# A cached attention decode step: loads of both caches moved from two queues to one, in 8 MB pieces, with a ring for the keys

## The chip, the cores and the metric

One core of a Trainium2 chip runs the whole program. The metric is the device time of one execution in microseconds. Times here are medians of several runs, and a profile shows one further execution.

## The reference

`B` = 2 sequences, one new token each, `D` = 512; 32 query heads of `DH` = 128 share 8 key/value heads (4 to 1); the caches hold `SK` = 32,768 positions. All is float32.

```python
xn = layernorm(x)
q  = (xn @ wq) split into 32 heads            # wq: 512 x 4096
scores = q . k_cache * DH**-0.5               # k_cache: 2 x 8 x 32768 x 128
o  = softmax(scores) . v_cache                # v_cache: the same shape
s  = o (heads side by side) @ wo              # wo: 4096 x 512
h  = relu(xn @ w1 + b1)**2                    # w1: 512 x 1792
g  = silu(h @ w2 + b2)                        # w2: 1792 x 512
out = x + s * g                               # 2 x 512
```

Each cache is 268 MB, and every byte of both is read once. The weights add 24 MB.

## The kernel before

A **stretch** `s` (0 to 15) is one pair of key/value head and sequence, `hkv, b = divmod(s, B)`. Its 32,768 positions are cut into `NCH` = 4 chunks of 8,192: 4 MB of keys and 4 MB of values, 64 positions (32 KB) on each of 128 partitions.

**Loads.** Two pools hold two 4 MB buffers each: `kpool` for keys (and at the end for `wo`), `vpool` for values (and at the start for `wq`, `w1`, `w2`). A Python list `loads` fixes one order; `issue()` walks down it as long as the next load's pool has a free buffer, and `give(pool)` is called where a buffer's last reader has been written down. Keys and weights are issued from SP's DMA queue (`nc.sync`, `load_k` at L90, `load_w1` L101, `load_w2` L106, `load_wo` L113 to L118); values from ACT's (`nc.scalar`, `load_v` at L96). On the profile SP's queue is q1 and ACT's q10. Each queue issues in order; an issue waits in its queue until the readers of the buffer are done. The small inputs `b1`, `b2` and `x` are issued from SP ahead of `wq` (L72 to L74).

**Scores (L244, L249).** The products need keys with `DH` on the partitions, in blocks of 32. `nc.vector.transpose` turns 32 x 32 blocks; one instruction (L244) turns 1,024 elements per partition, 8 positions x 128. Eight of them do a chunk, into eight small tiles `kt`. TensorE multiplies each with the query, spread over a mask `qz` that POOL fills (L228), in products of 256 columns (L249); four products run side by side, one per group of 32 output partitions. A float32 product is two records in the profile.

**Softmax (L256 to L272).** When the fourth chunk's scores stand in PSUM: maximum on DVE (`rm`, L256), a transpose on TensorE (`mx_ps`, L258), small DVE steps (`mh`, `mm`, `nm`), then the exponential on ACT (`p`, L268). `probs` (L281 to L290) transposes `p` on TensorE into `pT_ps` and copies it to `pT` on ACT (two copies of 512 per stretch), and computes the scale `rs` per head.

**Values (L305 to L317).** For each 4 MB chunk 16 products of 512 columns add into `o_ps`; behind a stretch's last one `o_sb` is copied out, scaled and transposed into `oT`.

**Order.** A loop over `n` (chunks) writes down scores of chunk `n`, `probs` of the stretch before (at its first chunk), values of chunk `n - 4`, and `softmax` at the fourth chunk. The Tile framework builds each engine's list from this, and may set ready work ahead of work that waits; on the chip every engine goes through its list in order. `mlp_up` and `mlp_down` (the gate) come in at `n` = 1 and 2.

**End.** `project` (L379) multiplies `oT` by `wo`, heads 0 to 27 first; the last four heads go in three pieces of columns (`PIECES`), each followed by the product with `gate` (L389), a fold of the four partition groups on TensorE (L390) and a copy (L391); then one DMA writes the output (L392).

Of the kernel before, what the change touches and what calls it, by code (L numbers as in the profile page):

```python
# [9 lines left out]
F32 = mybir.dt.float32  # L10
# [4 lines left out]
P = 128  # L15

NG = 4
RUN = 64
CHUNK = P * RUN
NC = 2
NO = 8
KBUFS = 2
VBUFS = 2
PIECES = ((0, 256), (256, 384), (384, 512))
# [3 lines left out]
def gqa_decode_kernel(ctx: ExitStack, tc: tile.TileContext, x, kc, vc, wq, wo, w1, b1, w2, b2, out):  # L33
# [8 lines left out]
    NCH = SK // CHUNK  # L42
    FG = F // NG
    FJ = FG // 32
    WJ = 16
    SCALE = 1.0 / math.sqrt(DH)
    assert NC * 4 * REP == 32 and D == 512 and DH == P and REP * DH == 512 and NCH == 4 and F == P * FJ
# [5 lines left out]
    kpool = ctx.enter_context(tc.tile_pool(name="kpool", bufs=KBUFS))  # L53
    vpool = ctx.enter_context(tc.tile_pool(name="vpool", bufs=VBUFS))
    ktpool = ctx.enter_context(tc.tile_pool(name="ktpool", bufs=8))
# [11 lines left out]

    xt = const.tile([P, D], F32, name="xt")
# [4 lines left out]
    nc.sync.dma_start(b1t, b1.rearrange("(g f) -> g f", g=NG))  # L73
    nc.sync.dma_start(b2t, b2[None, :])  # L74

    tiles = {}
# [5 lines left out]
    def load_wq(i):  # L82
        t = vpool.tile([P, 2, wq.shape[1]], F32, tag="v", name=f"wq{i}")
        nc.sync.dma_start(t, wq.rearrange("(p d) f -> p d f", p=P)[:, 2 * i:2 * i + 2, :])
        return t

    def load_k(m):
        s, u = divmod(m, NCH)
        t = kpool.tile([P, RUN, DH], F32, tag="k", name=f"k{m}")
        nc.sync.dma_start(t, rows(kc, s).rearrange("(p t r) d -> p t r d", p=P, t=NCH)[:, u])  # L90
        return t

    def load_v(m):
        s, u = divmod(m, NCH)
        t = vpool.tile([P, RUN, DH], F32, tag="v", name=f"v{m}")
        nc.scalar.dma_start(t, rows(vc, s)[u * CHUNK:(u + 1) * CHUNK].rearrange("(p r) d -> p r d", p=P))  # L96
        return t

    def load_w1(_):
        t = vpool.tile([P, ND, F], F32, tag="v", name="w1")  # L100
        nc.sync.dma_start(t, w1.rearrange("(p d) f -> p d f", p=P))  # L101
        return t

    def load_w2(_):
        t = vpool.tile([P, FJ, D], F32, tag="v", name="w2")
        nc.sync.dma_start(t, w2.rearrange("(p j) e -> p j e", p=P))  # L106
        return t

    def load_wo(i):
        t = kpool.tile([P, WJ, D], F32, tag="k", name=f"wo{i}")  # L110
        src = wo[i * WJ * P:(i + 1) * WJ * P, :].rearrange("(j p) e -> p j e", p=P)
        if i == 0:
            nc.sync.dma_start(t, src)  # L113
        else:
            nc.sync.dma_start(t[:, :8, :], src[:, :8, :])
            nc.sync.dma_start(t[:, 8:12, :], src[:, 8:12, :])
            for c0, c1 in PIECES:
                nc.sync.dma_start(t[:, 12:, c0:c1], src[:, 12:, c0:c1])  # L118
        return t

    NK = NS * NCH
    loads = [("v", load_wq, 0), ("v", load_wq, 1)]
    for m in range(NK + NCH):
        if m < NK:
            loads.append(("k", load_k, m))
        if m == 1:
            loads.append(("v", load_w1, 0))
        if m == 2:
            loads.append(("v", load_w2, 0))
        if m >= NCH:  # L130
            loads.append(("v", load_v, m - NCH))
        if m == NK:
            loads.append(("k", load_wo, 0))
    loads.append(("k", load_wo, 1))
    free = {"k": KBUFS, "v": VBUFS}
    done = [0]

# [278 lines left out]
```

## Time and profile before

| | |
|---|---|
| time, three runs | 1342.0, 1342.37, 1343.8 us; median 1342.37 |
| span of the profiled execution | 1341.7 us |
| HBM read | 561.0 MB |
| packets on q1 (SP) and q10 (ACT) | 15,026 and 9,216 |
| key loads, value loads | 64 and 64, 4,096 KB each |
| DVE transposes (L244) | 512, 587.3 us busy in all |
| score products (L249) | 4,096 records, 372.5 us busy |
| value products (L305) | 2,048 records, 313.2 us busy |

The page of the profile lists each engine's busy time, then the span in 40 equal slices: a digit is the busy share of a slice in tenths, and below it stand the share of the 16 DMA engines and the GB/s that they moved. The chain that ended last is followed back from the last instruction to whatever released each step. A view by windows gives, for each stretch of time, busy time and instruction count per engine, the clock granted to TensorE, the DMA share and GB/s. A row of the timeline has start, duration, engine, line, operation, output<-input and count, and in brackets the idle time before it with what ended it. "x32" at a product means 32 records, which is 16 products.

### The profile page before, as it was taken

What the parts mean: (1) busy time and instruction counts of PE and PEld (TensorE: products, weight loads), DVE (VectorE), ACT (ScalarE), POOL (GpSimd) and SP (SyncE); (2) the same over time, 40 slices, a digit from 0 to 9 for tenths busy, and PEclk for the clock granted to TensorE, in tenths of its full rate; (3) what the DMA queues carried; (4) which work ended last, traced back from release to release, by engine and by line L of the source; (5) the groups of instructions that cost most, each with busy time, mean ns of one, the idle gap of its engine ahead of it and who ended that gap; (6) DMA issues with size and microseconds to landing.
All of it is one profiled execution on the core that took longest, in us unless ns stands there. A gap on an engine that the chain in (4) does not pass through costs nothing.

```text
span 1341.7 us, 15037 instructions
## 1 busy us (share of the span) xinstructions
PE 754.6 (56%) x6702; PEld 277.8 (21%) x6702; DVE 640.7 (48%) x673; ACT 70.4 (5%) x117; POOL 28.0 (2%) x141
## 2 busy tenths in 40 slices
PE   4666366566563456454736656373664637367564
PEld 1212122122221122211212221121221212122121
DVE  3746546455565464454554445455444545544000
ACT  0001000010000000001000000100000010000010
POOL 1000000000000000000000000000000000000000
PEclk9978678767787778786878868686886868788778
DMA  9999999999999999999999999999999999999994
GB/s 393 433 434 381 429 430 423 432 416 424 434 414 432 435 388 431 433 429 434 429 429 434 429 432 429 431 430 433 427 433 431 428 434 426 434 428 426 377 397 211
DMA packets 24305, 561.96 MB, mean 419 GB/s; under 512 B 2217, under 2 KB 3757, under 8 KB 7346
## 3 DMA queue, kind: packets, MB, share of 16 engines
q1 hardware_dynamic: 15026, 292.57, 51.2%
q10 hardware_dynamic: 9216, 268.44, 46.7%
q8 instruction: 52, 0.85, 0.3%
q14 instruction: 11, 0.09, 0.0%
HBM read 561.00 MB, written 0.00 MB: 418 GB/s over the span
## 4 chain that ended last, share of the span: by engine, by line
DMA 62%; PE 18%; DVE 16%; ACT 2%; issue 1%; DVEq 0%; SPq 0%; ACTq 0%
DMA k<-in_A_k_cache 36%; DMA v<-in_A_v_cache 22%; DVE kt L244 15%; PE o_ps L305 12%; PE sc L249 3%; DMA wo<-in_A_wo 3%; PE pT_ps L281 2%; ACT p L268 2%; DMA wq<-in_A_wq 2%; PE l_ps L286 0%; PE q_ps L205 0%; PE qT_ps L216 0%; PE oT_ps L316 0%; PE a_ps L379 0%; DVE mh L260 0%
## 5 line engine op out<-in xcount | busy, mean ns | idle before, releaser
L244 DVE STREAM_TRANSPOSE kt<-k 128x1024 f32<-128x1024 f32 x512 | 587.3, 1210 | 452.4 <-DMA k<-in_A_k_cache 282.9
L249 PE MATMUL sc<-kt,qz 128*32 128x256 f32 x4096 | 372.5, 399 | 144.8 <-DVE kt L244 141.5
L305 PE MATMUL o_ps<-v,pT 128*16 128x512 f32 x2048 | 313.2, 754 | 201.1 <-DMA v<-in_A_v_cache 201.1
L249 PEld LDWEIGHTS sc<-kt,qz 128*32 128x32 f32 x4096 | 155.1, 113 | 360.7 <-DVE kt L244 218.5
L305 PEld LDWEIGHTS o_ps<-v,pT 128*16 128x16 f32 x2048 | 65.1, 114 | 413.2 <-DMA v<-in_A_v_cache 225.8
L281 PE MATMUL pT_ps<-ident,p 128*128 128x128 f32 x128 | 28.6, 395 | 196.4 <-ACT p L268 196.4
L281 PEld LDWEIGHTS pT_ps<-ident,p 128*128 128x128 f32 x128 | 22.7, 206 | 201.3 <-ACT p L268 200.9
L312 ACT COPY o_sb<-o_ps 128x512 f32<-128x512 f32 x16 | 9.4, 587 | 802.7 <-PE o_ps L305 802.7
L228 POOL COPY qz<-qT 32x16 f32<-32x16 f32 x128 | 25.2, 200 | 1047.6 <-PE sc L249 1017.1
L268 ACT ACTIVATE p<-sc,nm 128x1024 f32<-128x1024 f32 x16 | 33.2, 2077 | 189.9 <-DVE nm L265 189.9
L256 DVE TENSOR_REDUCE rm<-sc 128x1 f32<-128x1024 f32 x16 | 19.6, 1225 | 47.6 <-PE sc L249 47.6
L288 DVE RECIPROCAL r<-l_ps 128x4 f32<-128x4 f32 x16 | 2.9, 183 | 54.0 <-PE l_ps L286 54.0
L260 DVE TENSOR_REDUCE mh<-mx_ps 128x4 f32<-128x128 f32 x16 | 4.2, 265 | 40.1 <-PE mx_ps L258 40.1
L282 ACT COPY pT<-pT_ps 128x512 f32<-128x512 f32 x32 | 18.5, 587 | 21.7 <-PE pT_ps L281 21.7
L316 PE MATMUL oT_ps<-rs,o_sb 128*128 128x4 f32 x128 | 18.5, 268 | 1.9 <-ACT o_sb L312 1.9
L316 PEld LDWEIGHTS oT_ps<-rs,o_sb 128*128 128x128 f32 x128 | 17.1, 208 | 10.3 <-issue 6.6
L389 DVE TENSOR_TENSOR a_sb<-gate,a_ps 128x128 f32<-128x128 f32 (+1 forms) x3 | 1.0, 325 | 35.9 <-PE a_ps L379 35.9
L379 PE MATMUL a_ps<-wo,oT 128*32 128x512 f32 (+2 forms) x80 | 10.6, 521 | 12.0 <-DMA wo<-in_A_wo 12.0
L205 PE MATMUL q_ps<-wq,xnT 128*32 128x512 f32 x64 | 10.6, 821 | 9.1 <-DMA wq<-in_A_wq 9.1
L272 DVE TENSOR_SCALAR lh<-selh,l 128x4 f32<-128x4 f32 x16 | 3.7, 229 | 24.2 <-ACT p L268 24.0
L212 DVE COPY qr<-q_ps 128x512 f32<-128x512 f32 x8 | 5.3, 690 | 19.5 <-PE q_ps L205 19.0
L317 ACT COPY oT<-oT_ps 128x4 f32<-128x4 f32 x16 | 2.7, 166 | 140.2 <-PE oT_ps L316 140.2
(66 smaller groups left out, 94.0 us busy)
## 6 DMA issues: line engine op xcount, KB each, us to landing
k<-in_A_k_cache SPq DMA_DIRECT2D x64, 4096.0 KB, 24.7
v<-in_A_v_cache ACTq DMA_DIRECT2D x64, 4096.0 KB, 27.7
wq<-in_A_wq SPq DMA_DIRECT2D x2, 4096.0 KB, 16.7
w<-in_B_w SPq DMA_DIRECT2D x2, 3584.0 KB, 33.6
wo<-in_A_wo SPq DMA_DIRECT2D x1, 4096.0 KB
wo<-in_A_wo SPq DMA_DIRECT2D x1, 2048.0 KB
wo<-in_A_wo SPq DMA_DIRECT2D x1, 1024.0 KB, 17.2
wo<-in_A_wo SPq DMA_DIRECT2D x1, 512.0 KB, 13.2
```

What stands on the lines that cost most here:

```text
L205: nc.tensor.matmul(q_ps[32 * g:32 * g + 32, f, :], xnT[:, d, 0:32], wqt[:, d2, cc * 512:(cc + 1) * 512], start=(d == 0), stop=(d == ND - 1))
L228: nc.gpsimd.tensor_copy(t[:, c, :, lo:lo + REP], qT[32 * a:32 * a + 32, b, hkv].rearrange("p h e -> p e h"))
L244: nc.vector.transpose(r.rearrange("p e o w -> p o e w"), kt[:, lo:lo + NO, :].rearrange("p o (e w) -> p o e w", e=4))
L249: nc.tensor.matmul(sc[s][32 * g:32 * g + 32, t // 2, c0:c0 + 256], qz[s % 2][:, c, e, :], kts[g][:, e].rearrange("p o w -> p (o w)"), star ...
L256: nc.vector.tensor_reduce(rm, sc[s], axis=AX.XY, op=ALU.max)
L268: nc.scalar.activation(p.rearrange("p o w t -> p o t w"), sc.pop(s).rearrange("p b (t o w) -> p o (b t) w", t=2, w=32), AF.Exp, bias=nm, s ...
L281: nc.tensor.transpose(t_ps[:, j * P:(j + 1) * P], p[:, 4 * i + j].rearrange("p w t -> p (w t)"), ident)
L282: nc.scalar.copy(sb[:, :, 4 * i:4 * i + 4, :].rearrange("p r o h -> p o r h"), t_ps.rearrange("p (o r h) -> p o r h", o=4, h=REP))
L305: nc.tensor.matmul(o[32 * g:32 * g + 16, :], pT[s][:, r0, 4 * i:4 * i + 4, :].rearrange("p o h -> p (o h)"), vt[:, lo:lo + 4, :].rearrange ...
L312: nc.scalar.copy(o_sb, o)
L316: nc.tensor.matmul(t_ps[:, :REP], o_sb[:, i * DH:(i + 1) * DH], r4[:, i, :], start=(i == 0), stop=(i == 3))
L379: nc.tensor.matmul(a_ps[32 * g:32 * g + 32, 0, c0:c1], oT[:, hq, :], wot[hq // WJ][:, hq % WJ, c0:c1], start=(hq < NG), stop=(hq >= HQ - 2 ...
```

## The change

The chunks become twice as large, and the loads go through one queue.

- **Half stretches.** A step `m` (0 to 31) is half a stretch: `RUN` = 128 positions per partition, 8 MB of keys and 8 MB of values, each partition's row 64 KB. A key step has two halves of `SLOT` = 64 positions.
- **Buffers.** `kring` holds three halves (12 MB); half `h` goes to slot `h % 3`. Where the two slots of a step are neighbours in order, one 8 MB load fills both, otherwise two 4 MB loads do. `vbuf` is one buffer of 8 MB for the values. `wq`, `w1`, `w2` are views of `vbuf`, `wo` is a view of the first two slots of `kring`, and small work tiles (`scratch`) come out of the `kt` pool, which has 4 tiles of twice the size instead of 8.
- **Queue.** All large loads are issued from SP, in an order written out by hand; `x`, the biases and `x4` (the token laid out on 4 x 2 partitions) from ACT. There is no list and no `give`: the order of the statements is the order of the queue.
- **Products.** One DVE transpose turns 32 of the 128 columns of 64 positions (2,048 elements per partition); score products have 512 columns, half as many as before. `probs` packs `pT` differently and makes eight ACT copies of 64 partitions x 256 per stretch in place of two.
- **Order.** In a step: scores of the first half, load of the next keys, scores of the second half, then `softmax` or `probs`, values of step `m - 2`, load of values `m - 1`, and `head_out` behind a stretch.
- **End.** Values 30 go to two slots of the ring. Values 31 are loaded in two halves, with `wo` between and behind them: heads 0 to 7, then the second half, then 8 to 15, 16 to 23, 24 to 27, 28 and 29, 30, 31. Heads 24 to 31 are multiplied in four pieces of 128 columns into four groups of partitions, so that the result has 128 columns on 8 partitions; `gate` and `x4` have the same layout. Two DMAs write the output.

```diff
+SLOT = 64
+RUN = 2 * SLOT
+NO = 16
...
+    kring = const.tile([P, 3 * SLOT, DH], F32, name="kring")
+    vbuf = const.tile([P, RUN, DH], F32, name="vbuf")
...
+    def load_k(m, halves=False):
+        a, b = slot(2 * m), slot(2 * m + 1)
+        src = k_rows(m)
+        if b == a + 1 and not halves:
+            nc.sync.dma_start(kring[:, a * SLOT:(b + 1) * SLOT, :], src)
+            return
+        for h in range(2):
+            load_k_half(m, h)
...
+    def load_v(j):
+        nc.sync.dma_start(vbuf, v_rows(j))
...
+    def load_wo(h0, h1):
+        nc.sync.dma_start(wo_t[h0 // 16][:, h0 % 16:h0 % 16 + h1 - h0, :],
+                          wo[h0 * P:h1 * P, :].rearrange("(h p) e -> p h e", p=P))
+
+    nc.sync.dma_start(wq_t, wq.rearrange("(p d) f -> p d f", p=P))
+    load_k(0)
...
-    nc.sync.dma_start(xt[:B, :], x2)
+    nc.scalar.dma_start(xt[:B, :], x2)
...
+    nc.sync.dma_start(w1_t, w1.rearrange("(p d) f -> p d f", p=P))
+    load_k_half(1, 0)
+    nc.sync.dma_start(w2_t, w2.rearrange("(p j) e -> p j e", p=P))
...
+    def scores(m, c):
+        s, u = divmod(m, 2)
+        if u == 0 and c == 0:
             sc[s] = big(f"sc{s}")
...
+        kt = kring[:, slot(2 * m + c) * SLOT:(slot(2 * m + c) + 1) * SLOT, :]
+        for e in range(4):
+            r = ktpool.tile([P, SLOT, 32], F32, tag="kt", name=f"kt{m}_{c}_{e}")
+            nc.vector.transpose(r, kt[:, :, 32 * e:32 * e + 32])
             for g in range(NG):
...
+                nc.tensor.matmul(sc[s][32 * g:32 * g + 32, u, :], qz[s % 2][:, c, e, :],
+                                 r[:, g * NO:(g + 1) * NO, :].rearrange("p o w -> p (o w)"),
+                                 start=(c == 0 and e == 0), stop=(c == 1 and e == 3))
...
+            for a in range(2):
+                for y in range(2):
+                    nc.scalar.copy(sb[64 * a:64 * a + 64, :, 4 * i:4 * i + 4, y, :].rearrange("p z o h -> p o z h"),
+                                   v[64 * y:64 * y + 64, :, :, a, :])
...
+    def values(j, vt, cs=(0, 1)):
...
+    def head_out(s):
...
+    def fold(dst, src, start, stop):
+        for j in range(4):
+            nc.tensor.matmul(dst[32 * j:32 * j + 32, 0:P], selg, src[:, j * P:(j + 1) * P], start=start, stop=stop,
+                             skip_group_check=True)
...
+    for m in range(NH):
+        s, u = divmod(m, 2)
+        if u == 0:
+            set_q(s)
+        if m == 1:
             mlp_up()
...
+        scores(m, 0)
+        if m == 0:
+            load_k_half(1, 1)
+        elif m + 1 < NH:
+            load_k(m + 1)
+            if m == 1:
+                mlp_down()
+                load_v(0)
+        scores(m, 1)
+        if u == 1:
             softmax(s)
...
+        if m >= 2:
+            if u == 0:
+                probs(s - 1)
+            values(m - 2, vbuf)
+            if m < NH - 1:
+                load_v(m - 1)
+            if u == 1:
+                head_out(s - 1)
+
+    A = NH - 2
+    nc.sync.dma_start(kring[:, SLOT:3 * SLOT, :], v_rows(A))
+    nc.sync.dma_start(vbuf[:, 0:SLOT, :], v_rows(A + 1)[:, 0:SLOT])
+    load_wo(0, 8)
+    nc.sync.dma_start(vbuf[:, SLOT:RUN, :], v_rows(A + 1)[:, SLOT:RUN])
+    load_wo(8, 16)
...
+    def heads4(h0, h1):
+        for hq in range(h0, h1):
+            for j in range(4):
+                nc.tensor.matmul(acc[32 * j:32 * j + 32, 0:P], oT[:, hq, :],
+                                 wo_t[hq // 16][:, hq % 16, j * P:(j + 1) * P],
+                                 start=False, stop=(hq == HQ - 1), skip_group_check=True)
+
+    probs(NS - 1)
+    values(A, kring[:, SLOT:3 * SLOT, :])
+    load_wo(16, 24)
+    load_wo(24, 28)
+    load_wo(28, 30)
+    load_wo(30, 31)
+    load_wo(31, 32)
+    values(A + 1, vbuf, (0,))
+    heads(0, 8)
+    values(A + 1, vbuf, (1,))
+    heads(8, 16)
+    head_out(NS - 1)
+    heads(16, 24)
+    asb = scratch("a_sb")[:, 0:D]
+    nc.vector.tensor_copy(asb, project)
+    fold(acc, asb, True, False)
+    heads4(24, HQ)
+    fin = const.tile([P, P], F32, name="fin")
+    nc.vector.tensor_mul(fin, gate, acc[:, 0:P])
+    nc.vector.tensor_add(fin, fin, x4)
+    for b in range(B):
+        eng = nc.sync if b == 0 else nc.scalar
+        eng.dma_start(out2[b, :].rearrange("(j e) -> j e", j=ND), fin[b:b + 97:32, :])
```

More of the change, by code (lines that the diff above doesn't have):

```diff
@@ L138, in issue @@
[L138 to L152 removed]
+    nc.gpsimd.memset(x4, 0.0)
+    nc.scalar.dma_start(xt[:B, :], x2)
+    nc.scalar.dma_start(b1t, b1.rearrange("(g f) -> g f", g=NG))
+    nc.scalar.dma_start(b2t, b2[None, :])
@@ L225, in set_q @@
             t = qz[s % 2][32 * a:32 * a + 32]
-            for c in range(NC):
+            for c in range(2):
                 lo = (c * 4 + a) * REP
```

270 lines of the change are left out of this document (82 added, 188 removed).

## The prediction

> **What bounds the kernel now.** I read the page first: busy engines, the slices, bytes read, the chain.
>
> ```profile
> PE 754.6 (56%) x6702; PEld 277.8 (21%) x6702; DVE 640.7 (48%) x673; ACT 70.4 (5%) x117; POOL 28.0 (2%) x141
> ...
> DMA  9999999999999999999999999999999999999994
> GB/s 393 433 434 381 429 430 423 432 416 424 434 414 432 435 388 431 433 429 434 429 429 434 429 432 429 431 430 433 427 433 431 428 434 426 434 428 426 377 397 211
> ...
> HBM read 561.00 MB, written 0.00 MB: 418 GB/s over the span
> ...
> DMA 62%; PE 18%; DVE 16%; ACT 2%; issue 1%; DVEq 0%; SPq 0%; ACTq 0%
> ```
>
> No compute engine is busy much over half the span; the DMA engines are at 9 in every slice but the last. So the question is what rate the stream has and where it falls short. Second view, the DMA queues in three windows: 5 to 35 us (only SP's queue at work), 500 to 1200 (steady) and 1245 to 1255 (only `wo`).
>
> ```profile
> DMA packets 442, 12.91 MB, mean 430 GB/s; under 512 B 48, under 2 KB 48, under 8 KB 48
> ...
> q1 hardware_dynamic: 442, 12.91, 99.7%
> ```
> ```profile
> DMA packets 10354, 301.32 MB, mean 430 GB/s; under 512 B 1140, under 2 KB 1140, under 8 KB 1140
> ...
> q10 hardware_dynamic: 5171, 150.83, 50.2%
> q1 hardware_dynamic: 5149, 149.98, 49.8%
> ```
> ```profile
> DMA packets 1916, 3.88 MB, mean 388 GB/s; under 512 B 23, under 2 KB 23, under 8 KB 1916
> ```
>
> One queue alone, with loads back to back, runs at 430 GB/s, no less than two together; 4 MB loads queued behind each other cost nothing at their seams. In the steady part the two queues carry 150.83 + 149.98 = 300.81 MB in 700 us, 429.7 GB/s. `wo`, in 2 KB rows, goes at 388.
>
> The bytes by shape: keys and values 536.87 MB, `wq` 8.39, `w1` and `w2` 7.34, together 552.6 MB in long rows; `wo` 8.39. At these rates 552.6/0.4297 = 1286.0 us and 8.39/0.388 = 21.6 us: **1307.6 us of streaming** in a span of 1341.7. The other 34 us lie here (windows, then timeline; the last two columns of a window are the DMA share and GB/s):
>
> ```profile
> 112.00:125.00 13.00, 11.93 (x104) 4.87 (x105) 12.23 (x17) 4.58 (x5) 0.00 (x0) 0.84 0.73 291
> 200.00:300.00 100.00, 62.09 (x524) 23.22 (x527) 54.86 (x61) 7.35 (x11) 1.60 (x8) 0.75 0.99 422
> 300.00:400.00 100.00, 62.39 (x601) 22.70 (x597) 58.01 (x57) 3.98 (x6) 3.21 (x16) 0.81 0.99 425
> 400.00:500.00 100.00, 48.76 (x463) 18.04 (x455) 50.98 (x51) 4.02 (x6) 1.60 (x8) 0.74 0.98 420
> 1260.00:1326.00 66.00, 39.46 (x285) 10.66 (x275) 1.35 (x7) 3.98 (x6) 0.00 (x0) 0.82 0.97 397
> 1325.00:1330.00 5.00, 2.61 (x16) 0.64 (x20) 0.00 (x0) 0.00 (x0) 0.00 (x0) 0.79 0.03 13
> ```
> ```profile
> 0.74 0.37 SPq L73 DMA_DIRECT2D b1t<-in_B_b  x1
> 1.73 0.84 SPq L84 DMA_DIRECT2D wq<-in_A_wq  x2
> 2.13 21.33 DMA wq<-in_A_wq
> 1327.39 5.32 PE L305 MATMUL o_ps<-v,pT 128*16 128x512 f32 x32 [4.43 <-DMA v<-in_A_v_cache]
> 1339.52 0.28 SPq L392 DMA_DIRECT2D out<-fin  x1
> ```
>
> Start 2.1 us (bytes flow 0.4 us after the issue at 1.73). The gap near 115: 13 x (1 - 291/430) = 4.2. 200 to 500: 100 x (8 + 5 + 10)/430 = 5.3. Near the end, values and `wo` waiting for buffers: 66 x 33/430 = 5.1. Then the tail: 0.03 of 5 us after 1325 puts the last byte at about 1325.2, and 16.5 us of compute follow. Sum 33.2 of 34.
>
> **The change part by part.**
>
> *Start.* `wq` becomes SP's first instruction (the small inputs go to ACT's queue): bytes from 0.74 + 0.4 = 1.2 us instead of 2.1. The layernorm then waits for `xt` behind long `wq` packets, but `wq` itself lands only near 22 us.
>
> *Rows of 64 KB.* A 32 KB row costs 700 x 16/(10,354 - 34 - 1,140) = 1.220 us (34 are other queues' packets), a 2 KB row 10 x 16/1,916 = 0.0835: a line through both leaves 8 ns fixed per row. Half as many rows save 0.3%, 4 us. No row of this trace is that long. Ends: -8 (twice the fixed part), and +7, the 0.6% by which the steady windows' two queues differ. I take -4, from the nearest row. The Trainium skill, "DMA: Bandwidth & Descriptors", Where 436 GB/s comes from, caps the ports at 435 GB/s; 552.6 MB at that rate would be 1270 us, an estimate, beyond my bound.
>
> *Steady state.* Per step m the one queue carries 8 MB of keys and 8 MB of values, 16.78/0.4297 = 39.0 us. Let T be the last byte of keys m. Values m-2 stream until T+19.5, keys m+1 until T+39.0. The queue is SP's, in order, so each issue must come before the bytes ahead of it run out. The durations:
>
> ```profile
> 990.49 9.13 DVE L244 STREAM_TRANSPOSE kt<-k 128x1024 f32<-128x1024 f32 x8 [7.58 <-DMA k<-in_A_k_cache]
> 1001.62 1.23 DVE L256 TENSOR_REDUCE rm<-sc 128x1 f32<-128x1024 f32 x1 [2.01 <-PE sc L249]
> 946.86 8.27 PE L305 MATMUL o_ps<-v,pT 128*16 128x512 f32 x64
> 971.20 6.14 PE L305 MATMUL o_ps<-v,pT 128*16 128x512 f32 x32 [4.88 <-DMA v<-in_A_v_cache]
> ```
>
> Landing to use is 2.2 us (1325.2 to 1327.39). Keys m+1 need the first half of keys m transposed: 4 transposes of twice the size. The elements are the same, so 9.13 for 4; were all of a transpose its start, 4.6; were strided reading dearer by half, 13.7. I take 9.13, the nearest row, as 4 or 13.7 leave the issue early too. T + 2.2 + 9.1 + 0.4 = T+11.7, 7.8 us early. Values m-1 need the single 8 MB buffer: the second half's transposes end at T+20.4, its products near T+21.7, when values m-2 have landed too; on softmax steps `rm` adds 1.2. The products of 8 MB take 8.3 us (x64 records) to 12.3 (2 x 6.14, low clock): released by T+31 to T+36, 3 to 8 us before T+39.0. So with one buffer and one queue **nothing runs dry**. What hides the wait is the other cache's 19.5 us load; without it each step would lose the values' 8.3 to 12.3 us.
>
> Halved score products (2,048 of 512 columns in place of 4,096 records of 256), fewer weight loads and `values` reordered touch only PE, which has room: 0. Eight ACT copies of 256 per `probs` replace two of 512:
>
> ```profile
> L282 ACT COPY pT<-pT_ps 128x512 f32<-128x512 f32 x32 | 18.5, 587 | 21.7 <-PE pT_ps L281 21.7
> L317 ACT COPY oT<-oT_ps 128x4 f32<-128x4 f32 x16 | 2.7, 166 | 140.2 <-PE oT_ps L316 140.2
> ```
>
> each between 0.166 and 0.587, about 0.38: 3.0 us, up from 1.2, beside the loads; they touch the end only through the 3 us of room above.
>
> Ring slots, weight views and half loads share tiles with what still runs. Waits go by region, not by tile:
>
> ```profile
> 1299.27 0.59 ACT L282 COPY pT<-pT_ps 128x512 f32<-128x512 f32 x1 [0.27 <-PE pT_ps L281]
> 1299.57 4.10 PE L305 MATMUL o_ps<-v,pT 128*16 128x512 f32 x32
> ```
>
> The product reads the first half of `pT` while the second is still being written. So sharing costs 0.
>
> *Early gaps* (4.2 + 5.3) and the mixing near the end (5.1) go with the order of need. `w1` waits for the query products, done by about 33 us, while `k0` streams until 40.
>
> *Tail.* `wo` is queued between and behind the last values, so small pieces of `wo` land last.
>
> ```profile
> 1332.84 0.59 ACT L312 COPY o_sb<-o_ps 128x512 f32<-128x512 f32 x1 [32.99 <-PE o_ps L305]
> 1333.48 1.05 PE L316 MATMUL oT_ps<-rs,o_sb 128*128 128x4 f32 x8 [0.76 <-ACT o_sb L312]
> ```
> ```profile
> L379 PE MATMUL a_ps<-wo,oT 128*32 128x512 f32 x56 | 8.1, 609 | 12.0 <-DMA wo<-in_A_wo 12.0
> L379 PE MATMUL a_ps<-wo,oT 128*32 128x128 f32 x16 | 1.4, 282 | 0.0
> L389 DVE TENSOR_TENSOR a_sb<-gate,a_ps 128x128 f32<-128x128 f32 (+1 forms) x3 | 1.0, 325 | 35.9 <-PE a_ps L379 35.9
> ```
>
> Behind the last half of the values come 6.3 MB of `wo`, 16.2 us. Beside them PE has that half's products (4.1 to 6.1), `head_out` (0.59 + 1.05 + 0.17), heads 8 to 24 (16 x 8.1/28 = 4.6), copy and fold (about 1.3) and seven narrow heads at up to 4 x 1.4/8 = 0.7 each: 17 to 19, against 16.2. That is level, or some 2.5 late; I take level, since the 0.7 is of products that stood alone between DVE's steps, and keep +2.5. After the last byte: landing 2.2, the last head 0.7, product with `gate` and sum 2 x 0.325, output from issue to end 1341.7 - 1339.5 = 2.2: 5.7 instead of 16.5.
>
> **Sum:** 1.2 + (1286.0 - 4) + 21.6 + 5.7 = 1310.5 us of span; the median before is 0.7 above its profiled span (1342.37 against 1341.7), so **1311 us**.
>
> **The rivals.** *Gaps at the softmax.* Before, the list puts the next keys' transposes ahead of the softmax:
>
> ```profile
> 1019.91 2.05 ACT L268 ACTIVATE p<-sc,nm 128x1024 f32<-128x1024 f32 x1 [17.13 <-DVE nm L265]
> 1022.02 1.97 PE L281 MATMUL pT_ps<-ident,p 128*128 128x128 f32 x8 [19.29 <-ACT p L268]
> ```
>
> PE stands 19 us behind a late `p`. Kept so, `p` comes at T+2.2+18.3+0.7+2.0 = T+23.2, `pT` at T+28.2, values end at T+40.5 at the low clock, the issue at T+40.9: 1.9 us x 15 steps = 28: **up to 1339**. At the full clock values end 4 us sooner and nothing is lost, so half of this case lies below 1330. Against: `softmax` now stands ahead of the values and has 15 us before the next keys.
>
> *Values behind the next keys (slower).* At the 10 steps whose next keys come as two 4 MB loads, PE's list may take the first half's products before values m-2. That half lands at T+29.3+2.2, its transposes end at T+40.6, values at T+48.9: the stream is empty from T+39.0 to T+49.3, 10 us x 10, **1414**. It decides from the point where values end after T+38.6. Against: in one queue the values always land first.
>
> *Long rows at equal pitch.* Were the rate that of the slowest steady window, 420 GB/s, 552.6 MB would take 1315.7 us: **1345**. Against: keys (pitch 128 KB) and values (32 KB) share the engines 49.8 to 50.2. The Trainium skill, same page, Latency and other measured facts, has copies with 512 KiB between rows at 207 GB/s where 214 is full; by that ratio the long rows would cost 43 us more, an estimate. No row here shows such a fall.
>
> *The change doesn't do what it says:* rows cut to 32 KB give 1315, inside the forecast's own range.
>
> **How the numbers follow.** Forecast 0.76 (1304 to 1318); softmax gaps 0.09, nearly all of it faster; values behind keys 0.09, slower; pitch 0.06, half of it within 0.2%, half slower. 0.2% is about what this measurement can tell. Faster 0.84, same 0.04, slower 0.12. The range goes from 1303 (the -8 end and a little less) to 1330; beyond it lie half of the softmax case and the two slower ones, 0.045 + 0.09 + 0.06, just under 0.2.
>
> **What would show it.** Right: GB/s near 430 in all slices from the second on, no early dip; SP's waits long, yet DMA share 1.00; half as many long packets; last `wo` byte some 5 to 6 us before the end. Wrong: windows of a step with a DMA share under 0.95 (values late), or share 1.00 at fewer GB/s (rows), or PE still at heads when the last piece lands.

## The result, and the profile after

The changed kernel takes **1314.17 us** (median of 4 runs, 1313.68 to 1315.37), the kernel before 1343.09 (4 runs, 1342.0 to 1345.11) on the same chip: a ratio of **0.9779, interval 0.9765 to 0.9793**. That is 28.9 us off. The profiled executions say the same, 1341.7 us of span before and 1312.8 after. A second set of runs of the changed kernel, made as the yardstick of the experiments, gave 1314.32.

The page of the changed kernel, the lines that answer to the first fence of the prediction, and the third part's line of the queue that brings the engines their instructions:

```profile
PE 717.0 (55%) x4698; PEld 154.9 (12%) x4698; DVE 621.2 (47%) x414; ACT 85.4 (7%) x213; POOL 27.6 (2%) x140
...
GB/s 416 420 440 442 420 442 428 430 438 426 436 424 442 432 436 424 444 424 428 434 439 432 421 448 426 431 439 430 436 420 442 428 435 432 432 428 429 435 420 289
...
q8 instruction: 37, 0.61, 0.2%
...
HBM read 561.01 MB, written 0.00 MB: 427 GB/s over the span
...
L235 ACT COPY pT<-pT_ps 64x256 f32<-64x256 f32 x128 | 46.9, 367 | 8.4 <-PE pT_ps L231 6.9
```

The bytes are the same and no engine is nearer to being the bound. The mean over the span went from 418 to 427 GB/s. The first slice went from 393 to 416, the dips to 381 and 388 are gone, and the last slice moved 289 instead of 211: the stream stops later in the span. (A slice is 33 us and a load of 64 KB rows is long, so slices swing between 420 and 448 here; that is the records' grain, as the windows below show.)

The steady rate, from the DMA queues in the window from 500 to 1200 us:

```profile
DMA packets 6079, 302.75 MB, mean 433 GB/s; under 512 B 672, under 2 KB 672, under 8 KB 672
...
q1 hardware_dynamic: 6054, 302.39, 100.0%
```

One queue instead of two, 6,079 packets instead of 10,354, and 302.39/700 = 432.0 GB/s instead of 429.7.

One step of the steady part, from the timeline (start, length, engine, line):

```profile
905.08 0.33 SPq L88 DMA_DIRECT2D vbuf<-in_A_v_cache  x1
...
916.98 17.66 DVE L198 STREAM_TRANSPOSE kt<-kring 128x2048 f32<-128x2048 f32 x8 [27.38 <-DMA kring<-in_A_k_cache]
...
925.90 0.33 SPq L72 DMA_DIRECT2D kring<-in_A_k_cache  x1
...
937.50 8.56 PE L254 MATMUL o_ps<-vbuf,pT 128*16 128x512 f32 x64
...
946.13 0.33 SPq L88 DMA_DIRECT2D vbuf<-in_A_v_cache  x1
...
955.83 17.66 DVE L198 STREAM_TRANSPOSE kt<-kring 128x2048 f32<-128x2048 f32 x8 [5.00 <-DMA kring<-in_A_k_cache]
```

With the prediction's 2.2 us from landing to use, the last byte of these keys came at T = 914.8. The next keys were issued at T+11.1 and the next values at T+31.3, when the products of the old ones had ended. The next keys' last byte came at T+38.8. So each issue came with some 8 us of bytes still ahead of it in the queue, or, if landing to use is as short as the end of the kernel before has it (below), with 9 to 10.

The end, in windows (busy time of each engine, granted clock, DMA share, GB/s) and in the timeline:

```profile
130.00:1270.00 1140.00, 622.44 (x4013) 129.51 (x4017) 550.41 (x352) 74.20 (x180) 20.64 (x104) 0.76 1.00 432
1270.00:1290.00 20.00, 12.01 (x100) 2.54 (x92) 0.00 (x0) 0.00 (x0) 0.00 (x0) 0.93 1.00 406
1290.00:1302.00 12.00, 8.24 (x56) 2.42 (x56) 0.00 (x0) 0.75 (x2) 0.00 (x0) 0.77 1.02 372
...
1302.00:1304.00 2.00, 1.22 (x8) 0.40 (x12) 0.00 (x0) 0.00 (x0) 0.00 (x0) 0.60 0.60 229
1304.00:1306.00 2.00, 2.00 (x12) 0.20 (x4) 0.00 (x0) 0.00 (x0) 0.00 (x0) 0.55 0.54 207
1306.00:1308.00 2.00, 1.18 (x40) 1.00 (x40) 0.69 (x1) 0.00 (x0) 0.00 (x0) 1.00 0.18 68
...
1307.00:1307.50 0.50, 0.50 (x20) 0.50 (x24) 0.00 (x0) 0.00 (x0) 0.00 (x0) 1.00 0.14 53
1307.50:1308.00 0.50, 0.50 (x28) 0.50 (x20) 0.00 (x0) 0.00 (x0) 0.00 (x0) 1.00 0.00 0
```
```profile
1302.78 3.40 PE L348 MATMUL a_ps<-kring,oT 128*32 128x512 f32 x16 [2.39 <-DMA kring<-in_A_wo]
...
1306.26 0.69 DVE L372 COPY a_sb<-a_ps 128x512 f32<-128x512 f32 x1 [44.93 <-PE a_ps L348]
...
1309.89 0.66 SPq L380 DMA_DIRECT2D out<-fin  x1
```

The stream is at a share of 1.00 until 1302. From there it does not stop, it thins out: 0.60, 0.54 and 0.18 of the 16 engines are busy while the last pieces of `wo` land. The engines that are still busy keep their rate (229/0.60 and 207/0.54 are 382 and 383 GB/s), so it is their number that falls. The two short windows put the last byte at about 1307.4; behind it come 5.4 us.

The kernel before had 14.7, not the 16.5 that the prediction read. A window counts a row where it starts, and its last row of 32 KB, 1.2 us long by the prediction's own division, starts behind 1325.75:

```profile
1325.75:1326.00 0.25, 0.00 (x0) 0.00 (x0) 0.00 (x0) 0.00 (x0) 0.00 (x0) 1.00 0.30 131
```

So the last byte came at about 1327.0, and the product that needed it began 0.4 us later, at 1327.39; the 2.2 us from landing to use are not in this trace. At the changed kernel's end the rows have 2 KB, and the error is under 0.1 us.

### The profile page after: what moved, and what is told of

It reads as the page before. It is cut to its first block, busy times and chain, and to the rows that moved or that the text cites. A ratio compares the mean times of both kernels' runs of the same rounds, so it can differ in the third digit from the quotient of the medians.

```text
span 1312.8 us, 10708 instructions
## 1 busy us (share of the span) xinstructions
PE 717.0 (55%) x4698; PEld 154.9 (12%) x4698; DVE 621.2 (47%) x414; ACT 85.4 (7%) x213; POOL 27.6 (2%) x140
## 2 busy tenths in 40 slices
DMA packets 15676, 561.70 MB, mean 428 GB/s; under 512 B 1399, under 2 KB 1419, under 8 KB 5518
## 4 chain that ended last, share of the span: by engine, by line
DMA 61%; DVE 14%; issue 12%; PE 10%; ACT 1%; SPq 1%; DVEq 0%; ACTq 0%
DMA kring<-in_A_k_cache 56%; DVE kt L198 13%; PE o_ps L254 7%; DMA vbuf<-in_A_v_cache 2%; DMA kring<-in_A_wo 2%; PE sc L200 1%; DVE rm L206 1%; ACT pT L235 1%; SPq L98 1%; PE oT_ps L266 0%; SPq L338 0%; PE pT_ps L231 0%; PE mx_ps L208 0%; ACT o_sb L262 0%; PE a_ps L348 0%
## 5 line engine op out<-in xcount | busy, mean ns | idle before, releaser
L198 DVE STREAM_TRANSPOSE kt<-kring 128x2048 f32<-128x2048 f32 x256 | 566.1, 2275 | 360.1 <-DMA kring<-in_A_k_cache 360.1
L200 PE MATMUL sc<-kt,qz 128*32 128x512 f32 x2048 | 379.0, 823 | 427.6 <-DVE kt L198 422.9
L254 PE MATMUL o_ps<-vbuf,pT 128*16 128x512 f32 x1984 | 252.5, 666 | 74.2 <-DMA vbuf<-in_A_v_cache 74.0
L200 PEld LDWEIGHTS sc<-kt,qz 128*32 128x32 f32 x2048 | 47.2, 124 | 733.9 <-DVE kt L198 588.3
L254 PEld LDWEIGHTS o_ps<-vbuf,pT 128*16 128x16 f32 x1984 | 56.9, 105 | 263.0 <-issue 167.4
L218 ACT ACTIVATE p<-sc,nm 128x1024 f32<-128x1024 f32 x16 | 18.9, 1183 | 936.1 <-DVE nm L215 936.1
L235 ACT COPY pT<-pT_ps 64x256 f32<-64x256 f32 x128 | 46.9, 367 | 8.4 <-PE pT_ps L231 6.9
L206 DVE TENSOR_REDUCE rm<-sc 128x1 f32<-128x1024 f32 x16 | 19.6, 1225 | 25.4 <-PE sc L200 25.4
L231 PE MATMUL pT_ps<-ident,p 128*128 128x128 f32 x128 | 18.1, 287 | 3.6 <-ACT p L218 3.6
L254 PE MATMUL o_ps<-kring,pT 128*16 128x512 f32 x64 | 9.2, 743 | 6.3 <-DMA kring<-in_A_v_cache 6.3
L348 PE MATMUL a_ps<-kring,oT 128*32 128x512 f32 x48 | 7.2, 733 | 4.2 <-DMA kring<-in_A_wo 4.2
## 6 DMA issues: line engine op xcount, KB each, us to landing
kring<-in_A_wo SPq DMA_DIRECT2D x2, 256.0 KB, 10.6
```

What stands on the lines that cost most here:

```text
L198: nc.vector.transpose(r, kt[:, :, 32 * e:32 * e + 32])
L200: nc.tensor.matmul(sc[s][32 * g:32 * g + 32, u, :], qz[s % 2][:, c, e, :], r[:, g * NO:(g + 1) * NO, :].rearrange("p o w -> p (o w)"), sta ...
L206: nc.vector.tensor_reduce(rm, sc[s], axis=AX.XY, op=ALU.max)
L218: nc.scalar.activation(p.rearrange("p o w u -> p u o w"), sc.pop(s).rearrange("p u (o w) -> p u o w", w=32), AF.Exp, bias=nm, scale=SCALE, ...
L231: nc.tensor.transpose(t_ps[:, j * P:(j + 1) * P], p[:, 2 * (4 * i + j):2 * (4 * i + j) + 2].rearrange("p y w u -> p (y w u)"), ident)
L235: nc.scalar.copy(sb[64 * a:64 * a + 64, :, 4 * i:4 * i + 4, y, :].rearrange("p z o h -> p o z h"), v[64 * y:64 * y + 64, :, :, a, :])
```

## The experiments

The theory: the 29 us are time in which the stream ran short. Most of it (the early gaps, the mixing near the end, the tail) goes because one queue carries the loads in order of need; the 64 KB rows give some 4 us; the halved products and the reordered `values` give nothing, since PE has room; the single value buffer costs nothing, since the other cache's load covers it. The rivals: that one queue, or fewer and larger loads, raise the rate by themselves; that the cover of the single buffer is thin or much wider than reckoned; that the order of the last weights doesn't matter. All ratios are to the kernel before.

**The same kernel again.**

> The changed kernel itself, as the control of this group. 1314 us (1313 to 1316), profile with 432 GB/s from 500 to 1200 us.

Measured 1314.32 us (4 runs, 1313.92 to 1315.92), 0.978 [0.9767, 0.9794]. A difference of 4 us between kernels below is well outside this spread.

**Rows of 32 KB, in two loads or in one.** In the first, every load of 8 MB is cut in two; in the second it stays one load, but each partition's row is two rows of 32 KB that lie apart in HBM (so keys meet other values than in the reference and the output differs; the work and the bytes are the same).

```diff
     def load_v(j):
-        nc.sync.dma_start(vbuf, v_rows(j))
+        for h in range(2):
+            nc.sync.dma_start(vbuf[:, h * SLOT:(h + 1) * SLOT, :], v_rows(j)[:, h * SLOT:(h + 1) * SLOT])
```
```diff
-        return rows(vc, s)[u * P * RUN:(u + 1) * P * RUN].rearrange("(p r) d -> p r d", p=P)
+        return rows(vc, s).rearrange("(w u p r) d -> p w u r d", w=2, u=2, p=P)[:, :, u]
...
-        nc.sync.dma_start(vbuf, v_rows(j))
+        nc.sync.dma_start(vbuf.rearrange("p (w r) d -> p w r d", w=2), v_rows(j))
```

The keys are changed likewise.

> The changed kernel with every 8 MB load of a cache cut into two 4 MB loads, each with rows of 32 KB; order and buffers unchanged. Theory (rows of 64 KB raised the rate from 429.7 to 432.0 GB/s): the rate falls back to about 429.7, 552.6 MB take 6.8 us longer, 1321 us. Rival 1 (the rate rose because one queue replaced two that interleave): 1314 us. Rival 2 (the number of loads counts, not the rows): 1321 us here as well, but not in a_32k_one.

> The changed kernel with 8 MB loads as before, but each partition's 128 positions come as two runs of 32 KB from two places of the cache. Keys and values are then paired with other positions than the reference pairs them; work and bytes are the same. Theory (row length sets the rate): 1321 us, as a_32k_two. Rival 1 (one queue): 1314 us. Rival 2 (number of loads): 1314 us, below a_32k_two.

Measured 1318.55 us, 0.9813 [0.9799, 0.9826], and 1318.84 us, 0.9815 [0.9802, 0.9829]: 4.2 and 4.5 above the yardstick, and equal to each other. The theory's 1321 was too high: from 500 to 1200 us the rate fell to 430.5 and 430.4 GB/s, not to the 429.7 of the kernel before. The queue's bytes from 130 to 1270 us (packets, MB, share), of the changed kernel, of the two loads and of the one:

```profile
q1 hardware_dynamic: 10004, 491.98, 99.9%
```
```profile
q1 hardware_dynamic: 16700, 490.71, 100.1%
```
```profile
q1 hardware_dynamic: 16074, 490.64, 100.1%
```

At the same share the same 1140 us move 1.3 MB less, which is 3.0 us of stream. So the length of a row counts here, and the number of loads that a queue is given does not.

**The kernel before, with one queue alone.**

```diff
-        nc.scalar.dma_start(t, rows(vc, s)[u * CHUNK:(u + 1) * CHUNK].rearrange("(p r) d -> p r d", p=P))
+        nc.sync.dma_start(t, rows(vc, s)[u * CHUNK:(u + 1) * CHUNK].rearrange("(p r) d -> p r d", p=P))
```

> The kernel before with the value loads issued from SP too, so one queue in the order of its list; 4 MB loads, rows of 32 KB and all else unchanged. Theory: the early gaps (about 9.5 us) and part of the mixing near the end (5 us) go, rate 429.7 and tail (16.5 us) stay: 1329 to 1334 us. Rival 1 (one queue raises the rate): about 1323 to 1327, with 432 GB/s from 500 to 1200 us. Rival 3 (a single in-order queue with 4 MB buffers stands behind waits): slower than 1343.

Measured 1324.67 us (4 runs), 0.9854 [0.9841, 0.9868]: 19.6 us of the 30.0 between the two kernels of this group come from this one word. It is more than expected, and the trace shows why. Windows, then timeline:

```profile
112.00:125.00 13.00, 11.77 (x94) 3.76 (x94) 7.16 (x7) 0.00 (x0) 0.00 (x0) 0.74 1.01 432
120.00:500.00 380.00, 251.57 (x1969) 87.66 (x1960) 185.89 (x192) 19.89 (x30) 8.00 (x40) 0.81 1.00 430
...
1314.00:1316.00 2.00, 2.00 (x25) 0.67 (x20) 0.00 (x0) 0.00 (x0) 0.00 (x0) 1.00 0.51 138
1316.30:1317.00 0.70, 0.14 (x8) 0.04 (x6) 0.42 (x1) 0.00 (x0) 0.00 (x0) 1.00 0.02 4
```
```profile
1291.41 0.33 SPq L96 DMA_DIRECT2D v<-in_A_v_cache  x1
1291.83 0.39 SPq L115 DMA_DIRECT2D wo<-in_A_wo  x1
...
1320.01 0.29 SPq L392 DMA_DIRECT2D out<-fin  x1
```

The early gaps are closed: 432 GB/s where there were 291, and 430 from 120 to 500 where the windows had shown 420 to 425. That is the 9.5 us of the prediction's early gaps. The other 10 are mostly the tail, which the expectation had left as it was: in one queue the last piece of `wo` stands behind the last values and so lands last, at about 1316.4, and 5.8 us of the 1322.2 follow it instead of 14.7. The last byte itself came 10.6 us earlier than in the kernel before, and the early gaps are 9.5 of these; so only about 1 of the 5 us of mixing near the end can have gone with this edit. The rate itself did not rise, from 500 to 1200 us:

```profile
q1 hardware_dynamic: 10326, 300.78, 100.0%
```

300.78 MB against 150.83 + 149.98 = 300.81 in two queues. The rival that one queue is faster in itself falls.

**Two queues in the changed kernel.**

```diff
     def load_v(j):
-        nc.sync.dma_start(vbuf, v_rows(j))
+        nc.scalar.dma_start(vbuf, v_rows(j))
```

> The changed kernel with the value loads of the loop issued from ACT's queue instead of SP's; sizes, buffers and order of the statements as they are. Then keys and values no longer queue behind each other: both loads in flight share the engines, and the keys of the next step can start while the values still stream, but the single value buffer is refilled only after its products. Theory (the order of need in one queue is what keeps the stream full: a value load issued 7.5 us early is covered by the keys behind which it stands): keys get ahead, land together with the values and then both buffers wait for the engines at the same time, so gaps of some us per step: 1330 to 1420 us. Rival (any second load in flight is cover enough, one queue is not needed): 1312 to 1318 us.

Measured 1400.95 us (4 runs), 1.0418 [1.0396, 1.0439]. The page's slices show where, and the timeline around 840 us shows how:

```profile
GB/s 421 420 446 276 420 438 357 424 434 420 391 421 421 419 421 446 364 419 445 417 433 417 334 423 447 421 393 442 425 422 429 438 334 441 396 421 392 243 286 316
```
```profile
834.77 9.99 PE L254 MATMUL o_ps<-vbuf,pT 128*16 128x512 f32 x64 [18.04 <-DMA vbuf<-in_A_v_cache]
...
839.61 6.70 DVE L198 STREAM_TRANSPOSE kt<-kring 128x2048 f32<-128x2048 f32 x3 [22.45 <-DMA kring<-in_A_k_cache]
```

Two loads in flight share the engines, so here keys and values came into use within 5 us of each other; PE and DVE have both stood idle for some 20 us and then work at the same time, and while they do, the loads that wait for their buffers wait together. That is about half of the loss: from 130 to 1270 us the two queues moved 251.59 + 220.46 = 472.05 MB against 491.98, some 46 us of stream out of 86.6. The rest lies at the two ends: at the start the share of the DMA engines was 0.09 and 0.01 in the windows 115 to 120 and 120 to 125 us, and in the last three slices the page has 243, 286 and 316 GB/s. With one value buffer the order in one queue is the change's foundation: with the same large loads and the values on a second queue the kernel is 4% slower than before.

**The value products twice, and three times.** The products of `values` in the loop are issued two or three times into the same sum, so the attention's sums come out doubled or tripled.

```diff
-                for g in range(NG):
+                for g4 in range(reps * NG):
+                    rep, g = divmod(g4, NG)
...
-            values(m - 2, vbuf)
+            values(m - 2, vbuf, reps=2)
```

> The changed kernel with every value product of the loop made twice (the output is then off, the loads and waits are the same). In the profile of the change the values' release comes about 7.5 us before the bytes ahead of it run out (issue at 946.1, stream until 953.6). Theory (the stream runs dry only from the point where values end after about T+38.6): doubling adds 7 to 9 us, so gaps of 0 to 1.5 us on the softmax steps alone, 1314 to 1337 us. Rival (no room: each us on TensorE counts on each of the 30 steps): about 1314 + 30 x 8 = 1550 us.

> The same with every value product made three times. Theory: 14 to 18 us more against 7.5 (softmax steps) and about 11 (steps with half loads): gaps of 7 to 10 us on the former and 3 to 6 on the latter, 30 steps: 1450 to 1560 us, with the empty stretches ahead of value loads. Rival (TensorE has room for any of it): below 1340 us.

Measured 1333.07 us (2 runs, 1331.0 and 1335.14), 0.9914 [0.9885, 0.9942], and 1568.94 us (2 runs), 1.1668 [1.1633, 1.1703], the latter a little above what was expected. The second set costs 19 us, the third 236 more: over the 30 steps of the loop 0.6 us each, then 7.9 each. A set of products that costs 7.9 us where nothing hides it cost 0.6, so about 7 us a step were room, as a rough estimate: a set lasts less than it costs here (20.78/3 = 6.9 us), and the 19 us are not all waits for the buffer. The load queue's share from 500 to 1200 us was 98.9%, which is 7.7 us of 700, and the page has 0.85 MB of instructions instead of 0.61, which costs something by itself (below). Three sets, in the timeline and in windows of 5 us:

```profile
1097.41 20.78 PE L255 MATMUL o_ps<-vbuf,pT 128*16 128x512 f32 x192
1118.25 0.33 SPq L88 DMA_DIRECT2D vbuf<-in_A_v_cache  x1
```
```profile
1105.00:1110.00 5.00, 5.00 (x52) 1.40 (x48) 0.24 (x1) 0.00 (x0) 0.00 (x0) 1.00 0.50 213
1110.00:1115.00 5.00, 5.00 (x52) 1.29 (x44) 0.00 (x0) 0.00 (x0) 0.00 (x0) 1.00 0.00 0
1115.00:1120.00 5.00, 5.00 (x52) 1.48 (x48) 0.88 (x1) 0.00 (x0) 0.00 (x0) 1.00 0.56 197
```

The queue runs dry soon after 1107 while PE is still at the products, which end at 1118.19, and bytes flow again only behind the issue at 1118.25. (A row of 64 KB is under way for 2.4 us, 65,536 bytes at a sixteenth of 432 GB/s, so windows as short as these place its bytes only roughly.) That is the failure that the prediction's two steady-state rivals described.

**The order of the last loads, three ways.** In one kernel the last half of the values goes behind all of `wo`; in one the pieces of `wo` that stand between the two halves go behind them; in one the heads 16 to 24 are taken with narrow products as the last eight are, behind the copy and the fold, so that PE keeps up with the last pieces.

```diff
     load_wo(0, 8)
-    nc.sync.dma_start(vbuf[:, SLOT:RUN, :], v_rows(A + 1)[:, SLOT:RUN])
     load_wo(8, 16)
...
     load_wo(31, 32)
+    nc.sync.dma_start(vbuf[:, SLOT:RUN, :], v_rows(A + 1)[:, SLOT:RUN])
```
```diff
-    nc.sync.dma_start(vbuf[:, 0:SLOT, :], v_rows(A + 1)[:, 0:SLOT])
+    load_v(A + 1)
     load_wo(0, 8)
-    nc.sync.dma_start(vbuf[:, SLOT:RUN, :], v_rows(A + 1)[:, SLOT:RUN])
     load_wo(8, 16)
```
```diff
-    head_out(NS - 1)
-    heads(16, 24)
...
-    heads4(24, HQ)
+    head_out(NS - 1)
+    heads4(16, HQ)
```

> The changed kernel with the last half of the values (4 MB) loaded behind all of wo instead of ahead of its last 24 heads. Theory (what is loaded last sets the tail): after the last byte come landing 2.2, products of that half 4.1 to 5.3, head_out 1.8, four heads 0.5 to 1, gate and sum 0.6, output 2.9: 12 to 14 us instead of 6.4, so 1320 to 1322 us. Rival (the tail is the output's own time and landing, whatever is last): 1314 us.

> The changed kernel with the last values loaded as one 8 MB load and all of wo behind it, instead of in two halves with heads 0 to 7 between them. Theory (only what lands last and what stands behind it counts; the 8 to 9 us of products of the last values are hidden behind 21.6 us of wo): 1314 us, within 1.5. Rival (putting weights between the values is worth something): 1318 us or more.

> The changed kernel with heads 16 to 23 multiplied in the narrow form too, so that copy and fold (1.1 us) go in the idle time before wo for them has landed, and only narrow products stand behind it. Theory (TensorE was late by about 1 to 2 us at the end: heads 16 to 23 at the low clock 3.4, copy 0.7, fold 0.4, narrow heads 1.8 in a row after 1302.8): 1312 to 1314 us. Rival (the landing of the last piece sets the end): 1314 to 1315 us.

Measured 1322.06 us, 0.9833 [0.9817, 0.985]; 1313.7 us, 0.977 [0.9754, 0.9786]; and 1313.9 us, 0.9772 [0.9756, 0.9789]. So what lands last is worth 8 us, and the weights *between* the halves are worth nothing. The last of the three cannot be told from the changed kernel. Its timeline says why:

```profile
1302.98 5.55 PE L354 MATMUL a_ps<-kring,oT 128*32 128x128 f32 x128 [1.78 <-DMA kring<-in_A_wo]
...
1308.11 0.16 PEld L354 LDWEIGHTS a_ps<-kring,oT 128*32 128x32 f32 x8 [0.25 <-DMA kring<-in_A_wo]
1309.24 0.66 SPq L379 DMA_DIRECT2D out<-fin  x1
```

PE has caught up and waits for the last piece, usable at 1308.1, about 0.5 us behind its last byte (the windows have 10 GB/s from 1307.5 to 1307.7 and none from there to 1308.0); the output is issued 0.65 us earlier than in the changed kernel. PE and the landing are level to about a microsecond.

**Score products of 256 columns again.**

```diff
+            for y in range(2):
                 for g in range(NG):
-                    nc.tensor.matmul(sc[s][32 * g:32 * g + 32, u, :], qz[s % 2][:, c, e, :],
+                    nc.tensor.matmul(sc[s][32 * g:32 * g + 32, u, 256 * y:256 * y + 256], qz[s % 2][:, c, e, :],
```

> The changed kernel with each 512-column score product made as two of 256 columns, as before the change. Theory (TensorE is off the path, the wider products bought nothing): 1314 us, within 1.5. Rival (products and their weight loads are part of the gain): 1317 us or more.

Measured 1318.79 us (4 runs, 1317.82 to 1319.17), 0.9807 [0.9787, 0.9826]. On the same chip the kernel with the plain tail ran 1313.56 to 1313.76. The theory missed: the halved products are worth some 4.5 us. The page, then the load queue and the instruction queue from 130 to 1270 us, then the last 64 products of the changed kernel and of this one:

```profile
PE 718.9 (55%) x6746; PEld 242.4 (18%) x6746; DVE 621.3 (47%) x414; ACT 85.4 (6%) x213; POOL 27.8 (2%) x140
...
q8 instruction: 53, 0.87, 0.3%
```
```profile
q1 hardware_dynamic: 9908, 490.90, 99.8%
q8 instruction: 46, 0.75, 0.3%
```
```profile
1307.25 1.93 PE L354 MATMUL a_ps<-kring,oT 128*32 128x128 f32 x64
```
```profile
1309.84 3.41 PE L355 MATMUL a_ps<-kring,oT 128*32 128x128 f32 x64
```

PE's busy time is the same to 2 us, so it isn't PE's work in the loop. What grew is the code: 2,048 more products and as many weight loads, 16 more packets in the instruction queue. And the load queue moved 1.1 MB less, 2.5 us of stream; the last byte came at 1310.1 instead of 1307.4, 2.7 us later. The other 1.5 us of the two profiled spans (1316.9 against 1312.8) lie at the very end, in the two rows: the granted clock was 0.50 while these products ran, and 1.00 in the changed kernel. Whether the runs that were not profiled had that too isn't known, so not all of the 4.5 us is shown to be the stream's.

**As many instructions that do next to nothing.** To part the number of products from their shape, 32 products of one column are put ahead of each step's first score products, 1,024 in all. Their results are overwritten.

```diff
+        if c == 0:
+            for j in range(32):
+                nc.tensor.matmul(sc[s][32 * (j % 4):32 * (j % 4) + 32, u, j:j + 1], qz[s % 2][:, 0, 0, :],
+                                 ident[:, 0:1], start=True, stop=True)
```

> The changed kernel with 32 products of one column added per step (1,024 in all, into score columns that are overwritten afterwards): the same number of added TensorE instructions as in a_scores_256, without its halved products, and hardly any work. a_scores_256 took 4.5 us longer although TensorE was no busier; its steady rate fell from 432.0 to 430.0 GB/s, and the queue that brings TensorE's instructions moved 0.87 MB instead of 0.61. Theory A (the instructions themselves are loaded by the same DMA engines, and engines with that extra work hold up every load): 1317 to 1320 us, with about 430 GB/s from 500 to 1200 us and 0.87 MB on q8. Theory B (products of half the width cost by themselves, by weight loads or on the operands' side): 1313.5 to 1315.5 us at 432 GB/s.

Measured 1318.49 us (5 runs, 1316.88 to 1320.28), 0.9813 [0.9799, 0.9826]: 4.2 above the yardstick, as with the narrow score products. The page, and the two queues from 130 to 1270 us:

```profile
PE 750.9 (57%) x6746; PEld 186.8 (14%) x6746; DVE 621.9 (47%) x414; ACT 85.0 (6%) x213; POOL 27.6 (2%) x140
...
q8 instruction: 53, 0.87, 0.3%
```
```profile
q1 hardware_dynamic: 9892, 490.38, 99.8%
q8 instruction: 45, 0.74, 0.3%
```

The same count of instructions, the same 0.87 MB of them, the same time, though the score products are those of the changed kernel. PE is busy 34 us longer, but the DMA share from 130 to 1270 us stayed at 1.00, and the stream moved 1.6 MB less at that share, 3.7 us. The last byte came at about 1310.5, 3.1 us later than in the changed kernel; this profile is of the fastest of the five runs (1316.88 us). So it is the added products and their weight loads that cost, whatever their width, and some 3 us of it is seen in the stream. The two kernels have the weight loads in common as well, so the loading of code is not parted from what a weight load does.

## Why the prediction came out as it did

**What bounds the kernel: right.** The stream was the bound, and by the prediction's rates it was short by some 34 us. The span fell by 28.9 us, against a forecast of 31.2. They are not 28.9 of those 34: the rate itself rose too.

**Start: right in the gain.** `wq` is SP's first instruction, at 0.73 us. Windows of 0.1 us find its first rows between 1.7 and 1.8 us, where the sum had 1.2, and in the kernel before between 2.7 and 2.8, where it had 2.1. So both numbers were read too early, and the gain is 1.0 against 0.9.

**Rows of 64 KB, -4: right in size when they are undone alone**, which costs 4.2 and 4.5 us. Not all rows were halved in number, as the term took it: 22 loads of keys and 2 of values still come as 4 MB in rows of 32 KB, a fifth of the two caches. And the gain does not stand by itself (below). The rival of the long rows at equal pitch did not occur: with 64 KB rows 128 KB apart for the keys the rate rose to 432.0 GB/s. The Trainium skill, "DMA: Bandwidth & Descriptors", Latency and other measured facts, has its loss for copies with 512 KiB between rows; no run here has such a pitch. Rows were not cut to 32 KB throughout either: the page counts 15,676 packets against 24,305.

**Steady state: right, and by the same steps.** Keys' issue at T+11.1 against 11.7, values' at T+31.3 against 31 to 36, the next keys' end at T+38.8 against 39.0. The doubled and tripled products put the point from which it decides near where the prediction had it, about 7 us on. Neither of the two steady-state rivals occurred: in the step shown the values' products ended at 946.1, and the next keys came into use only 9.8 us later, with nothing dry in between.

**"Halved score products ... touch only PE, which has room: 0": wrong.** It is the step that failed. PE did have room in the loop, and its busy time there was the same. Undone alone, the term is 4.2 to 4.5 us of run time, some 3 of them seen in the stream: the kernel before issued 2,004 product records and as many weight loads more, these instructions are loaded through the same DMA engines (their queue stands among them on the page), and here, where the DMA engines are never idle, the stream carries less beside them. That the loading is the reason is argued, not shown. The page had the line for it, which went unread: 0.85 MB in the instruction queue before, 0.61 after.

**ACT's eight copies: right**, 0.367 us each against 0.38, and hidden.

**Early gaps: right that the order of need takes them away**, shown by the queue alone. For the mixing near the end, 5.1 in the prediction, it isn't shown: only about 1 us of it can have gone with that edit. That this one edit also moves the tail, by about as much again, wasn't seen: the prediction put the tail down to the new place of `wo`, and in one queue `wo` comes last anyhow.

**Tail: right but for the stream's last bytes.** At 1302 us 2 x (229 + 207 + 68) GB/s = 1.01 MB were left. At 388 GB/s they would have landed at 1304.6, where the prediction had 1304.8. That the two agree is partly luck: long rows at 432.0 take 552.6/0.4320 = 1279.2 us, 2.8 less than forecast, and nearly as much was lost again, 0.5 by the later first bytes and 1.1 from 130 to 1270 us (491.98 MB in 1140 us are 431.6 GB/s); about 1 us is not placed. Then the engines finished unevenly, and the last byte came at 1307.4: 2.6 us late, a term that the sum did not have. Behind it came 5.4 us, with 5.7 forecast, and that is luck too: the 2.2 from landing to use are about 0.5 where PE waits for the last piece (1308.1, above), the output took 2.9 from its issue (1309.89 to 1312.8) instead of 2.2, and PE, at a granted clock of 0.55 to 0.60 from 1302 to 1306, was late by the 0.65 that the narrow heads won back. That is the 2.3 us between the forecast of the span, 1310.5, and 1312.8. PE was level with the landing to about a microsecond, as taken. That it is the last place that matters, and not the place of `wo` between the values, is shown by the three kernels of the last loads.

How the 30 us of the experiments' group split: 19.6 for the one queue. The other 10.4 cannot be parted into rows and instructions. The load queues from 500 to 1200 us:

| kernel | rows | instruction packets in the whole run | MB |
|---|---|---|---|
| changed | 64 KB, some 32 | 37 | 302.39 |
| rows in two loads; in one | 32 KB | 37 | 301.34; 301.30 |
| narrow scores; tiny products | 64 KB, some 32 | 53 | 301.01; 300.81 |
| before, in one queue | 32 KB | 52 | 300.78 |

Short rows alone take 1.05 to 1.09 MB, more instructions alone 1.38 to 1.58, and the kernel that has both only 1.61. So they do not add up: by these figures long rows were worth nearly nothing with as many instructions as before (the last kernel differs in more than these two, so this is an indication). 300.78 against 302.39 MB is 6.8 us over the 552.6 MB, for both together; some 3.6 of the 10.4 are left for the start and the end. No kernel here undoes both in the changed one.

**What stays open.** Why the instructions cost so much. 0.26 MB more, spread over 16 engines at 432 GB/s, would take 0.6 us, not 3 to 4. A packet of them takes longer than its bytes: in the window from 535 to 540 us of the changed kernel the instruction queue's one packet has 1.4% of 16 engines' time, 1.1 us, so sixteen more are an estimated 1.1 us of the stream, still not 3. That few of the engines carry them and hold up the rest would fit, and so would the uneven finish, but the records at hand give the mean of the 16 engines only, so neither was shown, and no kernel here tries it. Nor does one add weight loads without products, or the other way round.

## What to carry to other kernels

Where the DMA engines are never idle, look for every stretch in which the stream runs short, and set one queue in the order in which data is needed before spending memory on more buffers: one word gave two thirds of the gain here, and the same large loads without it lost 4%. A buffer is free to be single as long as its products end before the bytes queued ahead of its next load do: work that out as a time on one step's timeline, and test it by doubling the work. In such a kernel an edit that only spares some 4,000 instructions of an engine with room was worth 4 us: look at the instruction queue's line.

## What the runs showed of the hardware that was not expected

Instructions cost time on an engine that has room: 2,048 more products and their weight loads (0.26 MB) took 4.2 and 4.5 us in two kernels that had nothing else in common, and put the last byte of the stream 2.7 and 3.1 us back. Rows of half the length cost 1.05 to 1.09 MB of 302.39 in 700 us, these instructions 1.38 to 1.58, and a kernel with both only 1.61.

A stream that was never starved ends unevenly: the share of busy DMA engines fell through 0.60, 0.54 and 0.18 over the last 6 us, and the last byte came 2.8 us after a level end (1304.6 to 1307.4).

A small load issued behind long rows is slow. In the kernel before `x`, 4 KB, was in use 1.4 us after its issue (1.44 to 2.86), ahead of `wq` in SP's queue; here, on ACT's queue, it was 13.9 us, with `wq` in rows of 64 KB under way on SP's. From the timeline of the changed kernel:

```profile
1.62 0.26 ACTq L114 DMA_DIRECT2D early<-in_A_x  x1
...
15.54 0.69 DVE L140 TENSOR_REDUCE st<-early 128x1 f32<-128x512 f32 x1 [13.02 <-DMA early<-in_A_x]
...
22.99 8.45 PE L160 MATMUL q_ps<-vbuf,xnT 128*32 128x512 f32 x64 [2.02 <-DMA vbuf<-in_A_wq]
```

The layernorm's result was ready at 21.7 us and `wq` usable at 23.0, so 1.3 us of room were left there.
